# Attention and a Fourier mixing layer on one core: sums made ahead, another rounding instruction, a planner's allowance, and the order of the last products

## The chip, the core and the metric

The kernel runs on one core of a Trainium2 chip. The metric is device time in microseconds. The kernel before was timed three times; a further execution was profiled.

A core has PE (TensorE, matmuls), DVE (VectorE), ACT (ScalarE) and POOL (GpSimd); SP (SyncE) issues the DMAs here. Each engine takes its instructions in order.

## The reference

```python
# A: attention, S = 2048, D = 1024, 32 heads of 32
qkv = (x @ wqkv).reshape(B, S, 3, H, Dh).transpose(2, 0, 3, 1, 4)
scores = einsum("bhqd,bhkd->bhqk", q, k) * Dh ** -0.5
o = einsum("bhqk,bhkd->bhqd", softmax(scores), v)
a = o.transpose(0, 2, 1, 3).reshape(B, S, D) @ wo
# B: Fourier mixing, real part, with given matrices
ar = einsum("bsd,ed->bse", x, dft_hid_re); ai = einsum("bsd,ed->bse", x, dft_hid_im)
y = einsum("ts,bse->bte", dft_seq_re, ar) - einsum("ts,bse->bte", dft_seq_im, ai)
out = concatenate([a, y], axis=-1)
```

All inputs and outputs are float32.

## The kernel before

**Products.** Every large matrix product (q, k and v; dense1 and dense2 for the Fourier part; the projection with `wo`) is cut into 2 x 2 blocks and done with seven block products instead of eight. Each needs sums or differences of blocks as operands; products are numbered 1 to 7. dense1 runs them in the order `OUTER = (1, 2, 5, 6, 7, 4, 3)`; its products 1 and 3 (`SPLIT`) are themselves done with seven inner products. These two are called the split stages. The stationary operands of dense1 are blocks of B_x (`xb`), the moving ones blocks of the sequence matrices (`ct`).

**Rounding.** A float32 operand is split into a rounded part (fp32r, "high") and the rest ("low"), and each product is three matmuls: high x high, low x high, high x low. `halves` (line 543) makes both: the high part with a copy on DVE (line 550, in the trace a CAST) or, where `spare` is set, on ACT (line 549); the low part with a subtraction on POOL or DVE (line 553). `spare` is set in the first five stages of q, k and v (x < 5), in the split stages, and from `behind()` on in the projection. `piece` prepares a stationary operand, `moving` a moving one. `fetch` loads the blocks from DRAM, adds them (line 530, POOL or DVE) and can store the sum.

**Sums.** In dense1, `split_a` names the blocks whose sum a stationary operand is. `simple(p)` loads and adds them at the beginning of product p, when n = 0 (8 operands of 128 x 4 x 128); products 5 and 6 store their sums, since 6 is made from 5, and the third sums (for the split product 3) are made and stored within product 7. `split(i)` loads and adds the operands of its inner products itself, 2 for each.

**Attention.** For each head, scores are made twice: by rows (psS, line 1586), for the maximum (DVE, line 1592) and the sum of exponentials (ACT, line 1595), and transposed (psT, line 1711) for the exponentials that are used (ACT, line 1718) and then multiplied by v (line 1741). The maxima go through DRAM (`m_d`) into the operand of the transposed scores (qs). Attention runs from about 185 to 2762 us; the block products are filled in between its matmuls.

**The planner.** All instructions are recorded as operations with a duration, an engine and sometimes another engine with another duration and rank. At trace time `Plan` runs a clock and gives each engine its next operation by rank; the result is the written order of every engine's instructions. Its costs are constants: CAST 0.415, ACAST (a rounding on ACT) 0.63, ADD 0.68 (an addition on DVE), SUB 1.31 (on POOL). An operation marked `two` and any operation on POOL exclude each other in the plan, and such an order is kept on the chip by an added dependency. `MARGIN` adds to the expected landing of a load before an engine may be given what uses it: POOL 2, DVE 2 (3 while attention runs), ACT 0.

**The projection.** `project` runs its seven products in `ORDER` (1, 2, 7, 6, 5, 3, 4), 8 groups of 12 matmuls each, in slots of SBUF given by `WHERE`. Operands q(r, 0) come from heads 0 to 15, q(r, 1) from heads 16 to 31. `behind()` opens memory that is free only when all heads have been stored; before it, loads use the buffers of the earlier stages.

Of the kernel before, what the change touches and what calls it, by code (L numbers as in the profile page):

```python
# [224 lines left out]
def kernel(  # L225
# [154 lines left out]
    SUB = 1.31  # L380
    ISSUE = 0.46
# [161 lines left out]
    def halves(raw, made, users, hi, lo, old, mine, order=(None, None)):  # L543

        rank = seq()

        def high(e=None):
            if e == "ACT":
                return nc.scalar.activation(hi(), raw(), AF.Copy)
            return nc.vector.tensor_copy(hi(), raw())  # L550

# [3 lines left out]
        a = op("DVE", CAST, high, [made] + old[0], [users, mine[0]], 10 + rank, 0, order[0], ("ACT", ACAST, 25 + rank) if spare[0] else None, two=True)  # L555
# [85 lines left out]
    CR.users = [att_gate for _ in range(NCR)]  # L641

    def qkv():
# [269 lines left out]
        for x, (p, blocks, v) in enumerate(STEPS[:10]):  # L913
# [26 lines left out]
            for t in range(8 if v else 0):  # L940
# [5 lines left out]
                if t < 4 and x < 4:  # L946
                    load_v_weight(x + 1, t)
            where[0] = within
# [8 lines left out]
        for x in (10, 11):  # L957
            for t in range(8):
                v_group(x, t)
                if x == 11 and t < 4:  # L960
# [7 lines left out]
        for b in range(8):  # L968
            W = [piece(w_terms(p, lambda i, j: wqk[b + 8 * i][:, 4 * j : 4 * j + 4, :], None, None)) for p in (7, 4)]
            for n in range(2):  # L970
                qk_group(10, W[0], b, n)
                qk_group(11, W[1], b, n)

# [276 lines left out]
    def dense1():  # L1250
        s4 = [[[] for _ in range(2)] for _ in range(4)]
        t2 = [[[] for _ in range(8)] for _ in range(4)]
        s2 = [[[] for _ in range(2)] for _ in range(4)]
        s2_d = [[dram.tile([P, 4, P], F32, name=f"s2_d{m}_{k}") for k in range(2)] for m in range(4)]
        s4_d = [[dram.tile([P, 4, P], F32, name=f"s4_d{m}_{k}") for k in range(2)] for m in range(4)]
# [3 lines left out]
        s1, t1 = [[[] for _ in range(2)] for _ in range(4)], [[[] for _ in range(8)] for _ in range(4)]  # L1259
        s1_d = [[dram.tile([P, 4, P], F32, name=f"s1_d{m}_{k}") for k in range(2)] for m in range(4)]  # L1260
        t1_d = [[dram.tile([P, NB], F32, name=f"t1_d{n}_{c}") for c in range(8)] for n in range(4)]
        xq = lambda d, s: (xb[d, :, s : s + 4, :], [])
# [6 lines left out]
        def simple(p):  # L1269
            def a(m, k):  # L1270
                q = lambda r, kk: xq(4 * r + m, 8 * kk + 4 * k)
                return split_a(p, q, (s1_d[m][k], s1[m][k]), (s2_d[m][k], s2[m][k]))
# [5 lines left out]
            keep_a = {5: lambda m, k: (s1_d[m][k], s1[m][k]), 6: lambda m, k: (s2_d[m][k], s2[m][k])}.get(p, lambda m, k: None)  # L1278
            keep_b = {5: lambda n, c: (t1_d[n][c], t1[n][c]), 6: lambda n, c: (t2_d[n][c], t2[n][c])}.get(p, lambda n, c: None)
            A = {}  # L1280
            for n in range(4):
# [4 lines left out]
                def load(m, k):  # L1286
                    if n == 0:
                        A[m, k] = held(fetch([P, 4, P], a(m, k), keep_a(m, k)), None if m < 2 else 12 + 2 * m + k)
# [8 lines left out]
                for m in range(4):  # L1297
# [4 lines left out]
                    if p == 7 and 3 in SPLIT and m % 2:  # L1302
# [640 lines left out]
```

## Time and profile before

| | us |
|---|---|
| median of three runs | 2924.29 (2923.43 to 2924.42) |
| profiled execution | 2924.82 |
| its span | 2923.0 |
| PE busy | 2911.5 |
| DVE, ACT, POOL busy | 2260.2, 2297.2, 1107.2 |

The stages, found by counting the block products' matmuls in the trace: first five stages of q, k and v to 206 us (each some 40; stage x = 3 from 124, x = 4 from 162); the rest of q, k and v to 782; dense1's product 1 to 948, 2 to 1143, 5 to 1340, 6 to 1536, 7 to 1732, 4 to 1928, 3 to 2108; dense2 to 2767; the projection's products from then on, 22 us each. A share of busy time is read against such a stretch. The granted clock of PE is 1.00 throughout. A matmul's recorded duration contains its passage through the engine, so matmuls overlap in the record, and PE's rate is read from their starts.

### The profile page before, as it was taken

To read this page: it belongs to the slowest core of one execution; us is meant where nothing else is said; L and a number is where in the kernel's file an instruction comes from. 1 tells how busy PE (TensorE), PEld (TensorE's weight loads), DVE (VectorE), ACT (ScalarE), POOL (GpSimd) and SP (SyncE) were. 2 spreads that over 40 slices of the span, in tenths; PEclk is the share of its full clock that TensorE was granted. 3 is DMA by queue.
4 is the path that set the end of the run, shared out by engine and by line. 5 is a ranking of instruction groups with operands and counts; after the bars stand their busy time and mean duration, and the time that the engine had idled before them with its cause. 6 is when DMAs were issued, how large, how long until landed. Compare 5 with 4: busy or idle time off the path is not lost.

```text
span 2923.0 us, 46116 instructions
## 1 busy us (share of the span) xinstructions
PE 2911.5 (100%) x14826; PEld 2130.8 (73%) x14826; DVE 2260.2 (77%) x3072; ACT 2297.2 (79%) x4369; POOL 1107.2 (38%) x866
## 2 busy tenths in 40 slices
PE   9999999999999999999999999999999999999999
PEld 7887777776667776777776777777677777777787
DVE  7778888788889768777778787778877877876496
ACT  5348888888899888888888888988888888887532
POOL 2323335222365124243434342347613653342042
PEclk9999999999999999999999999999999999999999
DMA  9975658766687448678869775568735776663463
GB/s 340 372 241 186 201 183 280 231 214 223 220 263 227 146 136 274 219 241 273 277 224 286 227 240 170 155 192 281 231 98 172 255 238 189 188 189 123 124 241 140
DMA packets 444956, 636.24 MB, mean 218 GB/s; under 512 B 115726, under 2 KB 150286, under 8 KB 444590
## 3 DMA queue, kind: packets, MB, share of 16 engines
q1 hardware_dynamic: 444716, 633.29, 67.8%
q8 instruction: 120, 1.97, 0.3%
q14 instruction: 120, 0.98, 0.1%
HBM read 448.56 MB, written 184.57 MB: 217 GB/s over the span
## 4 chain that ended last, share of the span: by engine, by line
PE 94%; ACT 2%; DMA 2%; DVE 1%; issue 1%; SPq 0%; DVEq 0%; ACTq 0%
PE pd L433 43%; PE psT L1711 16%; PE psS L1586 15%; PE pd L1741 14%; PE psT L433 6%; ACT psS L1595 1%; ACT pt L1718 1%; DMA qs<-m_d 0%; DMA m_d<-lt 0%; DVE negm L1592 0%; DMA raw<-in_ct 0%; PE psT L455 0%; DMA er<-in_xa 0%; DMA qs<-qk_d 0%; DMA er<-in_wv 0%
## 5 line engine op out<-in xcount | busy, mean ns | idle before, releaser
L1592 DVE TENSOR_REDUCE negm<-psS 128x1 f32<-128x1024 f32 x1024 | 1242.4, 1220 | 255.9 <-PE psS L1586 244.6
L1595 ACT ACTIVATE psS<-psS,negm 128x1024 f32<-128x1024 f32 x1024 | 1230.0, 1201 | 75.2 <-DVE negm L1592 69.5
L1718 ACT ACTIVATE pt<-psT 128x512 f32<-128x512 f32 x1656 | 1000.8, 705 | 267.4 <-PE psT L1711 243.8
L433 PE MATMUL pd<-slot,h 128*128 128x512 f32 x2704 | 921.3, 390 | 0.0
L1711 PE MATMUL psT<-qs,ks 128*128 128x512 f32 x2048 | 794.5, 394 | 2.3 <-ACT pt L1718 1.3
L553 POOL TENSOR_TENSOR slot<-raw,slot 128x512 fp32r<-128x512 f32 x278 | 357.6, 1292 | 776.1 <-DVE slot L550 424.2
L433 PEld LDWEIGHTS pd<-slot,h 128*128 128x128 f32 x2704 | 507.5, 188 | 106.1 <-issue 0.8
L530 POOL TENSOR_TENSOR raw<-raw,g 128x512 f32<-128x512 f32 x321 | 414.8, 1302 | 428.4 <-issue 78.1
L433 PE MATMUL pd<-slot,l 128*128 128x512 f32 x1352 | 526.7, 390 | 0.0
L1711 PEld LDWEIGHTS psT<-qs,ks 128*128 128x128 f32 x2048 | 381.9, 188 | 142.0 <-issue 42.7
L1586 PE MATMUL psS<-ks,qs 128*128 128x512 f32 x1552 | 474.0, 391 | 2.5 <-ACT psS L1595 2.2
L433 PE MATMUL pd<-slot,slot 128*128 128x512 f32 x1560 | 436.3, 389 | 0.0
L1741 PE MATMUL pd<-pt,vt 128*32 128x512 f32 x3312 | 408.2, 594 | 0.0
L1586 PEld LDWEIGHTS psS<-ks,qs 128*128 128x128 f32 x1552 | 290.0, 188 | 67.0 <-ACT psS L1595 6.2
L433 PEld LDWEIGHTS pd<-slot,slot 128*128 128x128 f32 x1560 | 292.8, 188 | 60.8
L1595 ACT ACTIVATION_READ_ACCUMULATOR psS<-psS,negm 128x1 f32 x1024 | 328.2, 321 | 0.0
L433 PEld LDWEIGHTS pd<-slot,l 128*128 128x128 f32 x1352 | 253.8, 188 | 52.3
L1718 ACT ACTIVATE ptm<-psT 128x512 f32<-128x512 f32 x392 | 242.4, 716 | 48.9 <-PE psT L1711 47.1
L1741 PEld LDWEIGHTS pd<-pt,vt 128*32 128x32 f32 x3312 | 108.6, 110 | 231.8 <-issue 217.2
L553 POOL TENSOR_TENSOR l<-raw,h 128x512 fp32r<-128x512 f32 x105 | 135.5, 1290 | 224.5 <-PE psT L1711 79.0
L550 DVE CAST slot<-raw 128x512 fp32r<-128x512 f32 x364 | 168.0, 482 | 6.2 <-DMA raw<-in_wo 3.1
L1586 PE MATMUL psS<-ks,qx 128*128 128x512 f32 x496 | 150.1, 393 | 1.0 <-ACT psS L1595 1.0
(158 smaller groups left out, 2066.0 us busy)
## 6 DMA issues: line engine op xcount, KB each, us to landing
raw<-in_ct SPq DMA_DIRECT2D x212, 256.0 KB
g<-in_ct SPq DMA_DIRECT2D x148, 256.0 KB
raw<-ut_d SPq DMA_DIRECT2D x112, 256.0 KB
qk_d<-e SPq DMA_DIRECT2D x52, 512.0 KB
qs<-qk_d SPq DMA_DIRECT2D x128, 192.0 KB
ks<-qk_d SPq DMA_DIRECT2D x128, 192.0 KB
c<-xx_d SPq DMA_DIRECT2D x80, 256.0 KB
c<-u_d SPq DMA_DIRECT2D x72, 256.0 KB
```

The lines of the kernel that those rows point to most:

```text
L433: nc.tensor.matmul(box["ps"], a[1]((a[0].hi, a[0].lo)[u]()), b[1]((b[0].hi, b[0].lo)[v]()), start=k == 0, stop=k == n - 1)
L530: return (nc.gpsimd if e == "POOL" else nc.vector).tensor_tensor(out=dest(), in0=x, in1=y, op=ALU.add if sign > 0 and not turned else ALU. ...
L550: return nc.vector.tensor_copy(hi(), raw())
L553: return (nc.gpsimd if e == "POOL" else nc.vector).tensor_tensor(out=lo(), in0=raw(), in1=f(hi()), op=ALU.subtract)
L1586: nc.tensor.matmul(p[:, i * NB : i * NB + NB], (QX[0] if own else QS[h % 2])[:, qt * P : qt * P + P], KS[h % 2][:, c * 1024 + i * NB : c * ...
L1592: nc.vector.tensor_reduce(out=ST["negm"][:, c, qt : qt + 1], in_=box["p"], axis=AX.X, op=ALU.max, negate=True)
L1595: nc.scalar.activation(box["p"], box["p"], AF.Exp, bias=ST["negm"][:, c, qt : qt + 1], accum_out=ST["sums"][:, c, qt : qt + 1])
L1711: nc.tensor.matmul(box["p"], KS[h % 2][:, t * P : t * P + P], QS[h % 2][:, j * NB : j * NB + NB], start=True, stop=True)
L1718: nc.scalar.activation(box["t"], box["p"], AF.Exp)
L1741: nc.tensor.matmul(po["p"][j * DH : j * DH + DH, :], VT[h][:, k, :], box["t"], start=(k == t0), stop=(k == t), tile_position=(0, j * DH),)
```

## The change

It does five things.

1. `halves`: where `spare` is set, the high part on DVE is made by a `tensor_reduce` with the maximum over an axis of one element instead of `tensor_copy`. In the plan it costs SLOW = 0.6 and is not marked `two`.
2. `presum` makes a stationary sum of dense1 with `fetch` and stores it in DRAM; `BESIDE` says beside which stage: the 8 of the inner product operands of product 1 beside stage x = 3, the 8 sums of product 5 beside v's products 7 and 4, the 8 of product 6 beside the q and k products 7 and 4, those of 7 and the third ones (16) beside product 2, the inner ones of product 3 (8) beside product 4. `simple` and `split` then load one finished operand.
3. In the projection product 7 goes second. Its operands' differences, which product 6 uses again, go to DRAM (`s7_d`, `t7_d`) and are loaded again; `behind()` comes with the loads of product 2; slots are dealt anew.
4. `MARGIN["ACT"]` is 3 while attention runs, else 0.
5. The separate sums `s1`, `s2`, `s4` and their stores fall away.

```diff
@@ halves
+        one = spare[0]
         def high(e=None):
             if e == "ACT":
                 return nc.scalar.activation(hi(), raw(), AF.Copy)
+            if one:
+                return nc.vector.tensor_reduce(out=hi(), in_=wide(raw()), op=ALU.max, axis=mybir.AxisListType.X)
             return nc.vector.tensor_copy(hi(), raw())
+        def wide(t):
+            return t.rearrange("p (n o) -> p n o", o=1) if len(t.shape) == 2 else t.rearrange("p b (n o) -> p b n o", o=1)
-        a = op("DVE", CAST, high, ..., two=True)
+        a = op("DVE", SLOW if one else CAST, high, ..., two=not one)
@@ new, ahead of qkv
+    def presum(key):
+        what, i, m, k = key
+        if key in sums_of:
+            return
+        if i in (6, 3):
+            presum((what, {6: 5, 3: 6}[i], m, k))
...
+        terms = split_a(i, q, sums_of.get((what, 5, m, k), ()), sums_of.get((what, 6, m, k), ()))
+        to = sums_of[key] = dram.tile([P, 4, P], F32, name=f"sum{what}_{i}_{m}_{k}"), []
+        fetch([P, 4, P], terms, to)
+    BESIDE = {"x":of_inner(1),"v":of_all(5),"qk":of_all(6),2:of_all(7)+of_all(3),4:of_inner(3)}
@@ simple
+                if p in (5, 6, 7, 3):
+                    presum(("s", p, m, k))
+                    return [(1, *sums_of["s", p, m, k])]
...
-                    if p == 7 and 3 in SPLIT and m % 2:
-                        i, k = divmod(2 * n + m // 2, 2)
-                        fetch([P, 4, P], [(1, *xq(i, 8 + 4 * k)), (-1, s2_d[i][k], s2[i][k])], (s4_d[i][k], s4[i][k]))
+                    beside(p, 1)
@@ project
-                6: lambda: [(1, A22[j][c]), (-1, S2[j][c])],
+                6: lambda: [(1, A22[j][c]), (-1, *S7[j][c])],
-        ORDER = (1, 2, 7, 6, 5, 3, 4)
+        ORDER = (1, 7, 2, 6, 5, 3, 4)
-                    Y[i // 2] = accs(12 + i // 2)
+                    Y[i // 2] = accs(g[1] + i // 2)
-                    if n != 2:
+                    if n == 2:
+                        behind()
+                        load_a(n, J0 + J1)
+                    elif n != 7:
                         load_a(n, J0)
                 if x == i == 0:
-                    load_a(2, J0 + J1)
+                    load_a(7, J0)
@@ the plan's loop
+        pl.MARGIN["ACT"] = 3 if heads and t_on[0] else 0
```

## Rows read from the trace of the kernel before

**Rows 1.** The page, part 1: busy us (share of the span) xinstructions

```profile
PE 2911.5 (100%) x14826; PEld 2130.8 (73%) x14826; DVE 2260.2 (77%) x3072; ACT 2297.2 (79%) x4369; POOL 1107.2 (38%) x866
```

**Rows 2.** The chain that ended last, its end: start us, us, what

```profile
2911.16 5.44 PE pd L433 x24
2916.60 2.73 PE psT L433 x12
2919.36 0.42 DVE e L1050
```

**Rows 3.** All waits of PE: who, awaited, us in total, times, longest us

```profile
PE psS L1586 <- ACT psS L1595: 3.2, 9, 0.6
PE pd L1817 <- DVE qs L312: 1.5, 1, 1.5
PE psT L1711 <- ACT pt L1718: 1.3, 2, 1.1
PE psT L1711 <- DMA qs<-m_d: 0.8, 2, 0.5
PE psT L455 <- DVE acc L821: 0.7, 1, 0.7
```

**Rows 4.** Timeline: start us, us, instruction, idle before it and releaser

```profile
717.36 0.63 ACT L549 ACTIVATE slot<-raw 128x512 fp32r<-128x512 f32 x1 [0.76 <-DMA raw<-in_ct]
718.52 0.50 PE L1711 MATMUL psT<-qs,ks 128*128 128x512 f32 x1 [0.27 <-ACT pt L1718]
...
799.61 0.63 ACT L549 ACTIVATE slot<-raw 128x512 fp32r<-128x512 f32 x1 [1.50 <-DMA raw<-in_ct]
800.78 0.50 PE L1711 MATMUL psT<-qs,ks 128*128 128x512 f32 x1 [1.08 <-ACT pt L1718]
```

**Rows 5.** Casts on DVE: dense1 products 1 and 3, then line 550 min/median/max

```profile
L550 DVE CAST slot<-raw 128x512 fp32r<-128x512 f32 x32 | 14.6, 479 | 0.9 <-DMA raw<-in_ct 0.9
...
L550 DVE CAST slot<-raw 128x512 fp32r<-128x512 f32 x39 | 19.8, 526 | 0.0
...
L550 DVE CAST slot<-raw x364: 382/419/1375, 188.3 to 2743.6; 128x512 fp32r<-128x512 f32 x182
```

**Rows 6.** Reductions on DVE and an addition on POOL: duration of one

```profile
L1592 DVE TENSOR_REDUCE negm<-psS 128x1 f32<-128x1024 f32 x1024 | 1242.4, 1220 | 255.9 <-PE psS L1586 244.6
...
L1619 DVE TENSOR_REDUCE lh<-negm x32: 178/186/189, 235.8 to 2686.5; 128x16 fp32r<-128x32 f32 x32
...
L530 POOL TENSOR_TENSOR raw<-raw,g x321: 1269/1289/1788, 259.9 to 2670.2; 128x512 f32<-128x512 f32 x161
```

**Rows 7.** Timeline before stage x=4: a weight load, an addition

```profile
136.18 0.43 SPq L511 DMA_DIRECT2D er<-in_wqk  x1
...
154.68 0.68 DVE L530 TENSOR_TENSOR er<-er,raw 128x512 f32<-128x512 f32 x1
```

**Rows 8.** Busy us by stretch: length, PE PEld DVE ACT POOL, clock, DMA, GB/s

```profile
124.00:162.00 38.00, 38.00 (x169) 31.49 (x168) 25.25 (x33) 11.58 (x19) 11.50 (x9) 1.00 0.86 310
162.00:205.00 43.00, 43.00 (x191) 35.60 (x190) 32.80 (x44) 16.73 (x29) 6.41 (x5) 1.00 0.75 250
782.00:948.00 166.00, 164.84 (x842) 119.04 (x841) 145.27 (x208) 152.12 (x293) 106.03 (x84) 1.00 0.78 242
1928.00:2108.00 180.00, 178.67 (x941) 125.28 (x940) 151.37 (x208) 158.03 (x306) 118.63 (x93) 1.00 0.81 254
2686.00:2767.00 81.00, 81.00 (x455) 54.80 (x454) 31.55 (x65) 40.17 (x75) 1.28 (x1) 1.00 0.36 110
2767.00:2788.00 21.00, 21.00 (x94) 17.38 (x94) 12.34 (x18) 8.84 (x14) 5.59 (x4) 1.00 0.88 306
2788.00:2810.00 22.00, 22.00 (x98) 17.93 (x97) 21.86 (x29) 8.84 (x16) 8.96 (x7) 1.00 1.03 370
```

**Rows 9.** The chain around a transfer of a head's maxima

```profile
550.79 5.50 DMA m_d<-lt
```

**Rows 10.** Waits of PE within dense1's product 3, 1928 to 2108 us

```profile
PE psS L1586 <- ACT psS L1595: 1.3, 4, 0.6
```

More of the change, by code (lines that the diff above doesn't have):

```diff
@@ L549, in high @@
                 return nc.scalar.activation(hi(), raw(), AF.Copy)
+            if one:
+                return nc.vector.tensor_reduce(out=hi(), in_=wide(raw()), op=ALU.max, axis=mybir.AxisListType.X)
             return nc.vector.tensor_copy(hi(), raw())
+        def wide(t):
+            return t.rearrange("p (n o) -> p n o", o=1) if len(t.shape) == 2 else t.rearrange("p b (n o) -> p b n o", o=1)
         def low(e):
             return (nc.gpsimd if e == "POOL" else nc.vector).tensor_tensor(out=lo(), in0=raw(), in1=f(hi()), op=ALU.subtract)
-        a = op("DVE", CAST, high, [made] + old[0], [users, mine[0]], 10 + rank, 0, order[0], ("ACT", ACAST, 25 + rank) if spare[0] else None, two=True)
+        a = op("DVE", SLOW if one else CAST, high, [made] + old[0], [users, mine[0]], 10 + rank, 0, order[0], ("ACT", ACAST, 25 + rank) if spare[0] else None, two=not one)
         b = op("POOL", SUB, low, [a] + old[1], [users, mine[0], mine[1]], rank, 0, order[1], other=("DVE", ADD, 25 + rank), two=True)
@@ L641, with of_all, of_inner, beside @@
     CR.users = [att_gate for _ in range(NCR)]
+    xq = lambda d, s: (xb[d, :, s : s + 4, :], [])
+    sums_of = {}
+    def presum(key):
[4 more added lines that the diff above has]
+            presum((what, {6: 5, 3: 6}[i], m, k))
+        if what == "s":
+            q = lambda r, kk: xq(4 * r + m, 8 * kk + 4 * k)
+        else:
+            q = lambda r, kk: sums_of["s", 3, 2 * r + m, kk] if what == 3 else xq(2 * r + m, 8 * (what - 1) + 4 * kk)
+        terms = split_a(i, q, sums_of.get((what, 5, m, k), ()), sums_of.get((what, 6, m, k), ()))
+        to = sums_of[key] = dram.tile([P, 4, P], F32, name=f"sum{what}_{i}_{m}_{k}"), []
+        fetch([P, 4, P], terms, to)
+    def of_all(p):
+        return [("s", p, m, k) for m in range(4) for k in range(2)]
+    def of_inner(i, ps=(5, 6, 7, 3)):
+        return [(i, p, n, 0) for p in ps for n in range(2)]
+    BESIDE = {"x":of_inner(1),"v":of_all(5),"qk":of_all(6),2:of_all(7)+of_all(3),4:of_inner(3)}
+    def beside(what, n):
+        todo = BESIDE.get(what, [])
+        for key in todo[:n]:
+            presum(key)
+        del todo[:n]
     def qkv():
@@ L959, in qkv @@
                 v_group(x, t)
+                if t % 2:
+                    beside("v", 1)
                 if x == 11 and t < 4:
@@ L972, in qkv @@
                 qk_group(11, W[1], b, n)
+                beside("qk", 1)
     ORDER = (1, 2, 6, 7, 5, 3, 4)
@@ L1502, in project @@
         T2 = [kept(f"t2_{c}") for c in range(4)]
+        S7 = [[(dram.tile([P, NB], F32, name=f"s7_d{j}_{c}"), []) for c in range(4)] for j in range(2)]
+        T7 = [(dram.tile([P, NB], F32, name=f"t7_d{c}"), []) for c in range(4)]
         def load_b(p):
             for c in range(4):
-                B[p, c] = moving(WHERE[p][1] + c, b_terms(p, c), None, T2[c] if p in (6, 7) else None)
+                B[p, c] = moving(WHERE[p][1] + c, b_terms(p, c), T7[c] if p == 7 else None, T2[c] if p == 6 else None)
         def load_a(p, which):
```

40 lines of the change are left out of this document (18 added, 22 removed).

## Prediction

> **What bounds the kernel now.** The page's first part comes first: PE (the matrix engine) is busy for 2911.5 of 2923.0 us [rows 1]. The change alters neither the number nor the shape of the matmuls, so it can win no more than PE's idle time, 2923.0 - 2911.5 = 11.5 us. Next, the end of the chain [rows 2]: the last matmul ends at 2916.60 + 2.73 = 2919.33, and 3.7 us of evacuation and storing follow, the same two half-tile steps after the change. The list of PE's waits [rows 3] has 1.5 us before the first matmul, also unchanged, and 6.0 us in 14 waits. A wait costs more than its idle time: a matmul is recorded for 0.390 us, but 24 of them take 5.44 us in the chain [rows 2], 0.227 each, so a wait moves the next start by its idle time and 0.163 more. The 14 waits cost 6.0 + 14 x 0.163 = 8.3 us; one of them, 0.7 + 0.16 on an accumulator, is in the first 20 us, which the change leaves alone. What is left, 7.4 us, is the most that this change can return: 0.25% of the time. Of these 13 waits 11 are on ACT (3.2 us for score exponentials, 1.3 for the transposed ones), two on a small DMA. So the question of each edit is which of these waits it takes away, and whether it makes one of its own.
>
> **Allowance on ScalarE.** Two waits can be followed to their cause in the timeline [rows 4]. At 799.61 ACT starts a rounding after standing idle for 1.50 us until that tile's load lands; the exponential queued behind it is late, and PE waits 1.08 us at 800.78. At 717.36 the same with 0.76 us, and PE waits 0.27. Both are roundings of dense1's product 1, taken by ACT at the very moment at which the planner expected the load. With MARGIN 3 the planner gives ACT such a tile only 3 us after the expected landing, more than either lateness. The gain is 1.08 + 0.27 + 2 x 0.163 = 1.7 us at most, nothing at worst (DVE, which already has an allowance, gets the tile, and its maxima stand ahead of the same exponentials). I take 1.7, for the cause is visible in both rows.
>
> **Rounding as a maximum over one element.** In the stages where ACT may help (`spare`), DVE's cast becomes a TENSOR_REDUCE. It applies to 45 casts in 782 to 948 us and to 49 in 1928 to 2108, of which [rows 5] show the two largest groups (32 at 479 ns, 39 at 526; the rest lie in smaller groups of 419 to 500), and to 13 in the first 205 us. A cast left alone takes 419 ns, but up to 1375 [rows 5]: it has to wait while POOL works. The reduce that reads SBUF was never over 189 ns in 32 cases [rows 6], so it does not wait for POOL. Its price for 512 outputs is not in the trace. From 1220 ns for 1024 elements and 186 for 32 [rows 6], one element costs 1034 / 992 = 1.04 ns, so 512 cost 186 + 480 x 1.04 = 0.69 us. The bounds are 0.42 (a cast alone) and 1.22 (a reduce of twice the input); I take 0.69, which is also nearest to an addition with 512 outputs, 0.68 us [rows 7]. DVE then has 45 x (0.69 - 0.48) = 9.5 us more in product 1, 145.3 + 9.5 = 154.8 of 166, and 49 x (0.69 - 0.51) = 8.8 more in product 3, 151.4 + 8.8 = 160.2 of 180 [rows 8]. Both still fit, so I cost it at nothing on PE. In return POOL's additions and subtractions (1.29 us each [rows 6]) can run beside a rounding.
>
> The Trainium skill speaks against this edit: "VectorE: DVE Perf Modes", section "Rules for kernel authors", says to expect the single rate of `tensor_reduce` and to restructure around it. By that rule alone DVE only loses, nothing of the 1.0 us that I count below for product 3 would come, and the time would be 2923.1. The page "SBUF — State Buffer", section "SBUF: two separate sides", has the counterweight: DVE's two-port modes and GpSimd exclude each other. The cast's spread of 382 to 1375 ns agrees with it.
>
> **Sums made ahead.** 48 sums of B_x blocks were made where they are used; now each is made earlier, stored, and loaded when used. The additions stay 48, but 8 of them leave each split stage: 8 x 1.29 = 10.3 us of POOL's 106.0 and 118.6 us there [rows 8], and 12 transfers leave each as well. In all, 56 transfers of 256 KB are added (8 loads each for the sums of products 5 and 6, 8 stores and 8 loads for product 7's, 12 for each split product; product 3's outer sums were stored and loaded before too), 14.7 MB. The full rate is 370 GB/s [rows 8], 0.71 us each. Most of it goes into stages with room. The tight place is the first: 8 sums for product 1 go into 124 to 162 us, 24 transfers or 17.0 us on top of 0.86 x 38 = 32.7, which overfills the stretch by 11.7 us; the next has 0.75 x 43 = 32.3 and takes it up to 44.0 of 43. Those loads go ahead of stage x = 4's weight blocks in the ring of load buffers. The last such block is loaded at 136.18, and the last addition on one runs at 154.68 [rows 7], so some 15 us of lead cover 17 of delay. I cost it at 0.2 us, between 0 and 5 (nothing else is ready for PE at 162). Elsewhere a busier queue lengthens small transfers on which PE waits, such as a head's maxima, 5.50 us at 550.79 [rows 9]; the two DMA waits, 0.8 us idle in all [rows 3], may grow by 0.2.
>
> What ACT, DVE and POOL get back in the split stages should show in product 3, where PE has 4 waits on ACT with 1.3 us idle [rows 10]: 1.3 + 4 x 0.163 = 1.95 us. ACT is only 158.0 of 180 us busy there, but in runs of exponentials without a gap, which fewer roundings on ACT break up only in part. Bounds 0 and 1.95; I take half, 1.0.
>
> **Product 7 second in the projection.** Both first products now use heads 0 to 15 alone, so 43 us of matmuls rather than 22 cover the last heads' store and load. But PE had no wait there: busy 21.00 of 21 and 22.00 of 22 [rows 8]. The gain is nothing. The cost: products 1 and 7 are prepared before `behind()`, so without ACT's roundings (8.84 us in 2767 to 2788). By 2788 DVE and POOL must do 12 casts, 12 low parts and 8 subtractions, 12 x 0.42 + 20 x 0.69 = 18.8 us if DVE does all, beside 8 evacuations of 0.69: 24.3 us in the 26 after attention ends near 2762. Before that they are little used (31.55 and 1.28 of 81). It just fits, and POOL takes some; I cost it at 0.1, between 0 and 3. In exchange DVE, which was full at 2788 to 2810 (21.86 of 22), has product 2's plain roundings there. The 12 stores and 12 reloads of S7 and T7 (17 us of transfers) fall where DMA has room and before product 6.
>
> **The sum.** -1.7 - 1.0 + 0.2 + 0.2 + 0.1 = -2.2 us. The profiled execution took 2924.82 us, 1.8 more than its span; it becomes 2922.6. The median of the three runs lies 0.5 below the profiled one: 2922.1.
>
> **Rivals.** *The waits are only dealt anew.* The planner places all later instructions again once a cost changes; waits go here and come there, or DVE's maxima come later by what ACT's exponentials gain. For it: 5 of the 11 waits on ACT lie outside both sets of rows, with no edit near. Time 2924.3, give or take 2.5. This is also where the change does not do what it says. *All waits go.* POOL and ACT have slack enough that nearly all of the 7.4 us vanish, 2917. Against it: the waits outside the split stages have other causes. *The one-element maximum is dear.* In the split stages, DVE is full when a rounding takes 0.48 + 20.7 / 45 = 0.94 us in product 1 (166 - 145.3 = 20.7 free) or 0.51 + 28.6 / 49 = 1.09 in product 3. At 1.22 it overruns by 45 x 0.74 - 20.7 = 12.6 and 49 x 0.71 - 28.6 = 6.2 us; if ACT's slack takes half, PE loses 9.4: slower, 2922.1 + 9.4 = 2931.5. Only a price for each output makes it so; the two reduces, with 1 and 16 outputs, hardly tell, and the addition with 512 speaks against it. *The run-up in the first stage* at its bound, 5 us, gives 2927.
>
> **How the numbers follow.** Forecast 2920 to 2924: 0.50. Dealt anew, 2922 to 2927: 0.25. All waits go: 0.12. Dear maximum: 0.08. Run-up: 0.05. The range leaves out half of the third and all of the fourth: 2917 to 2928. 0.2%, about what a measurement of this kernel can tell from no change, is 5.8 us: faster means under 2918.4, slower over 2930.1. Faster 0.11, same 0.80, slower 0.09.
>
> **What would show it.** In the changed profile: the waits at 717 and 800 gone and no ACT rounding with idle time on a DMA in attention; TENSOR_REDUCE on line 550's successor at 0.6 to 0.7 us without spread; POOL busy in product 1 and 3 about 10 us less; DMA near full from 124 to 205 with PE at 43.00 of 43; no wait of PE after 2767. It is wrong if the reduce is over 0.9 us, if PE waits near 162 or 2788, or if as many waits on ACT stand elsewhere.

## The result and the profile after

The change makes the kernel slower by 0.2%: 2930.95 us (median of 13 runs, 2927.28 to 2935.98) against 2925.45 for the kernel before, run beside it (13 runs, 2922.22 to 2942.39). The ratio is 1.002, 95% interval 1.0011 to 1.0028. The forecast was 2922.1 in a range of 2917 to 2928; the time lies outside it.

The profiled execution took 2933.52 us, 2.6 more than the median; its span is 2931.5, 8.5 more than before. Lines have moved: the block products' matmuls are on 434 and 456 (433 and 455 before), psS on 1629, psT on 1754, the product with v on 1784, the reduction for rounding on 553, the cast on 554, ACT's rounding on 551, the low part on 560. Part 1 of the page of the changed kernel, to be held against [rows 1]:

```profile
PE 2915.4 (99%) x14826; PEld 2131.0 (73%) x14826; DVE 2257.3 (77%) x3079; ACT 2277.8 (78%) x4326; POOL 1150.0 (39%) x902
```

The number of matmuls is the same. PE's idle time has gone from 11.5 to 2931.5 - 2915.4 = 16.1 us, and its busy time is up by 3.9, so matmuls also ran slower. Where it waits, beside [rows 3] (all waits of PE in the changed kernel: who, awaited, us in total, times, longest):

```profile
PE psS L1629 <- ACT psS L1638: 3.6, 5, 1.3
PE psT L1754 <- DMA qs<-m_d: 3.2, 2, 1.8
PE pd L1860 <- DVE qs L312: 1.5, 1, 1.5
PE pd L1784 <- DVE e L794: 1.4, 1, 1.4
PE psT L434 <- POOL l L560: 0.8, 1, 0.8
PE psT L434 <- ACT h L551: 0.8, 1, 0.8
PE psT L456 <- DVE acc L860: 0.4, 1, 0.4
PE psT L434 <- DVE l L560: 0.3, 1, 0.3
```

The two waits on transposed exponentials are gone, and the nine on score exponentials are five, though longer ones (3.6 us in all, 3.2 before). New are three waits within the first block products (L434), one in the product with v (L1784), and the two on a head's maxima have grown from 0.8 to 3.2 us.

**At 162 us.** The beginning of stage x = 4 in the timeline of the changed kernel (start, us, instruction, idle time before it and its releaser):

```profile
154.11 0.67 SPq L512 DMA_DIRECT2D er<-in_wqk  x1
154.83 0.77 SPq L521 DMA_DIRECT2D raw<-sum  x1
...
161.38 0.69 DVE L531 TENSOR_TENSOR er<-er,raw 128x512 f32<-128x512 f32 x1
162.10 0.63 ACT L551 ACTIVATE h<-er 128x512 fp32r<-128x512 f32 x1 [14.62 <-DVE er L531]
162.79 0.49 PE L434 MATMUL psT<-slot,h 128*128 128x512 f32 x1 [0.77 <-ACT h L551]
164.13 0.50 PE L434 MATMUL psT<-slot,l 128*128 128x512 f32 x1 [0.85 <-POOL l L560]
```

A weight block is issued at 154.11. Before, the last three of this stage were issued at 132.53, 133.58 and 136.18 (the last: [rows 7]); now they come at 154.11, 156.73 and 162.14, 22 to 26 us later. So the addition on it runs at 161.38, the rounding at 162.10, and PE waits for that rounding, then for its low part. The windows of the changed kernel tell why, and what follows (length; PE, PEld, DVE, ACT, POOL busy; granted clock; DMA share; GB/s):

```profile
124.00:162.00 38.00, 38.00 (x168) 31.17 (x166) 19.61 (x30) 5.41 (x9) 10.48 (x8) 1.00 0.97 341
162.00:209.00 47.00, 45.08 (x190) 36.48 (x190) 35.63 (x50) 20.31 (x34) 16.63 (x13) 0.96 0.93 332
165.00:169.00 4.00, 4.00 (x12) 3.13 (x12) 1.52 (x3) 1.02 (x2) 1.28 (x1) 0.62 1.06 406
480.00:539.00 59.00, 57.58 (x315) 37.93 (x314) 46.03 (x58) 46.62 (x88) 31.92 (x25) 1.00 0.97 322
539.00:586.00 47.00, 45.22 (x222) 33.20 (x221) 36.58 (x49) 39.68 (x78) 20.41 (x16) 1.00 0.93 304
787.00:952.00 165.00, 165.00 (x845) 119.47 (x843) 152.37 (x212) 146.12 (x282) 109.23 (x87) 1.00 0.71 227
1937.00:2104.00 167.00, 164.89 (x849) 117.12 (x848) 147.04 (x197) 143.15 (x276) 114.61 (x91) 1.00 0.81 255
```

DMA is at 0.97 and 0.93 where it was at 0.86 and 0.75 [rows 8]. And in the four microseconds behind the two waits the granted clock is 0.62 on average: the clock's record has half the clock, the 1.2 GHz level, from 164.65 on for 3.41 us. PE, which had run without a gap until 162, had just stood idle twice within 2 us. Eight matmuls then start every 0.427 us instead of 0.227: 1.6 us more. Stage x = 4 ends at 209.3 instead of 205.6.

**In the stages of v.** In the fourth and fifth line above v's products 7 and 4 are done; that is where the eight sums of dense1's product 5 are now made. In the kernel before, the same two stages read:

```profile
475.00:534.00 59.00, 59.00 (x307) 42.70 (x296) 48.31 (x61) 50.09 (x96) 29.86 (x24) 1.00 0.84 281
534.00:580.00 46.00, 45.66 (x225) 34.24 (x225) 34.61 (x46) 40.18 (x79) 13.46 (x11) 1.00 0.77 241
```

DMA went from 0.84 to 0.97 and from 0.77 to 0.93, PE lost 1.42 and 1.78 us. The first loss, in the timeline of the changed kernel:

```profile
527.00 0.33 SPq L824 DMA_DIRECT2D c<-u_d  x1
...
530.17 0.69 DVE L794 TENSOR_TENSOR e<-c,pd 128x512 f32<-128x512 f32 x1 [2.56 <-DMA c<-u_d]
...
530.91 2.35 PE L1784 MATMUL pd<-pt,vt 128*32 128x512 f32 x20 [1.38 <-DVE e L794]
```

The list of waits names DVE, but DVE had itself been waiting 2.56 us for a transfer: the partial sum `c`, read back from DRAM, lands late. DVE's addition frees the accumulator that the product with v needs next. The second loss is the wait for the maxima at 569.46 (1.75 us).

**In the projection.** No wait is left there. But its end in the chain of waits of the changed kernel (compare [rows 2], 5.44 us for 24 matmuls) reads:

```profile
2809.27 5.44 PE pd L434 x24
2814.71 5.53 PE psT L434 x24
2820.24 5.60 PE pd L434 x24
2825.84 5.56 PE psT L434 x24
2831.40 5.44 PE pd L434 x24
```

The same 24 matmuls take 5.53 to 5.60 us in a part of the products, with the clock at 1.00 and nothing awaited. By starts of matmuls, half a product (48) takes 10.88 us, but in products 2, 6, 3 and 4 one half takes 11.20: it is always the half whose stationary operand lies in slot 12. The half behind it takes 10.92. The projection takes 153.75 us; it was 152.57.

**The account.** From start to start of matmuls, changed minus before: the waits and the lower clock at 162 to 178, +4.4 (by the stage's end, 3.7); waits on maxima, +2.5; the wait in the product with v, +1.4; the projection's pitch, +1.4; small differences of under 0.03 us from one start to the next in the other stages, +1.2; waits on ACT in attention, -2.3. That is 8.6 of the 8.5.

This is the account of one execution; between the medians there are 5.5 us. Traces of other kernels that make the same sums beside the same stages show how much of it varies. The stretch from 140 to 213 us of the kernel before, by the same matmuls, is 4.0 us longer in the changed kernel, 4.1 in e2 below, but 1.9 in e4 and e14, where the waits in it are two of 0.5 to 0.6 us each; only the changed kernel has half clock there. In the stages of v, PE stands idle for 1.4 and 1.8 us in the changed kernel (L1784 and the maxima), 1.2 and 1.6 in e2, 1.4 and 2.1 in e4, 1.8 and 2.3 in e14.

### The profile page after: what moved, and what is told of

Same layout as the page of the kernel before. It is cut to its first block, busy times and chain, and to the rows that moved or that the text cites. A ratio compares the mean times of both kernels' runs of the same rounds, so it can differ in the third digit from the quotient of the medians.

```text
span 2931.5 us, 46241 instructions
## 1 busy us (share of the span) xinstructions
PE 2915.4 (99%) x14826; PEld 2131.0 (73%) x14826; DVE 2257.3 (77%) x3079; ACT 2277.8 (78%) x4326; POOL 1150.0 (39%) x902
## 4 chain that ended last, share of the span: by engine, by line
PE 91%; DMA 5%; DVE 2%; SPq 1%; issue 0%; ACT 0%; POOL 0%; DVEq 0%; ACTq 0%; POOLq 0%
PE pd L434 41%; PE psT L1754 15%; PE psS L1629 15%; PE pd L1784 15%; PE psT L434 5%; DMA c<-u_d 1%; DVE negm L1635 1%; DMA w_d<-raw 0%; DMA raw<-sums 0%; DMA er<-in_xb 0%; DMA sum<-er 0%; DMA sq_d<-er 0%; DMA qs<-qk_d 0%; DMA er<-in_xa 0%; DMA raw<-in_ct 0%
## 5 line engine op out<-in xcount | busy, mean ns | idle before, releaser
L1638 ACT ACTIVATE psS<-psS,negm 128x1024 f32<-128x1024 f32 x1024 | 1215.3, 1187 | 75.6 <-DVE negm L1635 70.1
L1761 ACT ACTIVATE pt<-psT 128x512 f32<-128x512 f32 x1656 | 989.8, 693 | 273.6 <-PE psT L1754 251.2
L434 PE MATMUL pd<-slot,h 128*128 128x512 f32 x2704 | 919.7, 390 | 0.0
L560 POOL TENSOR_TENSOR slot<-raw,slot 128x512 fp32r<-128x512 f32 x301 | 387.2, 1292 | 780.5 <-DVE slot L554 484.3
L434 PEld LDWEIGHTS pd<-slot,h 128*128 128x128 f32 x2704 | 507.6, 188 | 105.8 <-issue 0.8
L434 PE MATMUL pd<-slot,l 128*128 128x512 f32 x1352 | 526.6, 390 | 0.0
L434 PE MATMUL pd<-slot,slot 128*128 128x512 f32 x1584 | 445.0, 390 | 0.0
L1784 PE MATMUL pd<-pt,vt 128*32 128x512 f32 x3312 | 408.2, 594 | 1.4 <-DVE e L794 1.4
L434 PEld LDWEIGHTS pd<-slot,slot 128*128 128x128 f32 x1584 | 297.4, 188 | 61.5
L1629 PEld LDWEIGHTS psS<-ks,qs 128*128 128x128 f32 x1552 | 289.5, 188 | 69.1 <-ACT psS L1638 10.1
L1638 ACT ACTIVATION_READ_ACCUMULATOR psS<-psS,negm 128x1 f32 x1024 | 312.3, 305 | 0.0
L434 PEld LDWEIGHTS pd<-slot,l 128*128 128x128 f32 x1352 | 253.8, 188 | 52.5 <-POOL l L560 0.2
L1784 PEld LDWEIGHTS pd<-pt,vt 128*32 128x32 f32 x3312 | 108.5, 110 | 233.4 <-issue 217.4
L560 POOL TENSOR_TENSOR l<-raw,h 128x512 fp32r<-128x512 f32 x115 | 148.3, 1290 | 242.8 <-PE psT L1754 98.3
L554 DVE CAST slot<-raw 128x512 fp32r<-128x512 f32 x312 | 146.9, 489 | 6.0 <-DMA raw<-in_wo 2.9
```

The costliest lines, as they stand in the source:

```text
L434: nc.tensor.matmul(box["ps"], a[1]((a[0].hi, a[0].lo)[u]()), b[1]((b[0].hi, b[0].lo)[v]()), start=k == 0, stop=k == n - 1)
L560: return (nc.gpsimd if e == "POOL" else nc.vector).tensor_tensor(out=lo(), in0=raw(), in1=f(hi()), op=ALU.subtract)
L1629: nc.tensor.matmul(p[:, i * NB : i * NB + NB], (QX[0] if own else QS[h % 2])[:, qt * P : qt * P + P], KS[h % 2][:, c * 1024 + i * NB : c * ...
L1638: nc.scalar.activation(box["p"], box["p"], AF.Exp, bias=ST["negm"][:, c, qt : qt + 1], accum_out=ST["sums"][:, c, qt : qt + 1])
L1761: nc.scalar.activation(box["t"], box["p"], AF.Exp)
L1784: nc.tensor.matmul(po["p"][j * DH : j * DH + DH, :], VT[h][:, k, :], box["t"], start=(k == t0), stop=(k == t), tile_position=(0, j * DH),)
```

## The experiments

Each series ran on one chip beside the kernel before, whose median in it is given. "Sums" is part 2 of the change, "order" part 3.

**The parts by themselves** (before: 2925.43 for the first two, 2925.47 for the next two, 2924.79 for the last).

e2_sums_alone: the kernel before with `presum`, `BESIDE` and the loads of finished sums, nothing else.

> The kernel before with the sums made ahead, and nothing else of the change. Theory (the transfers of the sums cost the time): PE waits near 162 us by 1 to 2 us with a half-clock stretch behind it, waits on the maxima's transfer (qs<-m_d) are longer than before's 0.5 and 0.2, and the kernel is 4 to 8 us slower than before. Rival (the other edits cost it): no wait near 162 us, within 2 us of before.

e3_without_sums: the whole change without that part.

> The changed kernel without the sums made ahead: rounding as maximum, allowance on ACT and the projection's order stay. Theory (the transfers of the sums cost the time): no wait near 162 us, full clock, and 1 to 3 us faster than before, less 1.3 us in the projection if the slots there cost something. Rival (rounding or order cost it): still 3 us or more slower than before.

e7_rounding_alone: only the new instruction in `halves`.

> The kernel before with the rounding as one-element maximum alone. Theory (it fits, since DVE is not full): a reduce takes 0.68 us whether POOL works or not, within 2 us of before, and ACT does fewer roundings in the split stages. Rival (DVE is late by it): waits of PE on DVE or on ACT in the split stages, 3 us or more slower.

e8_allowance_alone: only this line.

```diff
+        pl.MARGIN["ACT"] = 3 if heads and t_on[0] else 0
```

> The kernel before with the allowance on ACT alone. Theory: the two waits near 718 and 801 us that come of a rounding on ACT waiting for its load are gone, no rounding on ACT waits for a transfer between 300 and 2700 us, 1 to 2 us faster than before. Rival (the plan is dealt anew): as many waits of PE on ACT as before in other places, no difference beyond 1 us.

e12_order_alone: only the projection's part, with its slots.

> The kernel before with product 7 second in the projection alone. Theory: everything before the projection as before, the wait of the third half product (11.13 us before) gone, -0.25 us, and four half products at 11.2 us in place of 10.88, +1.3 us: 1 us slower than before in the projection, 2926.5. Rival (preparing product 7 without ACT is late): waits of PE in product 7, 2 us or more slower.

| | median us | ratio to before (95%) |
|---|---|---|
| e2 sums alone | 2935.56 | 1.0032 (1.0019 to 1.0045) |
| e3 without sums | 2926.60 | 1.0003 (0.9993 to 1.0012) |
| e7 rounding alone | 2925.77 | 1.0002 (0.9993 to 1.0011) |
| e8 allowance alone | 2926.93 | 1.0005 (0.9996 to 1.0013) |
| e12 order alone | 2926.61 | 1.0005 (0.9996 to 1.0014) |

The loss is in the sums; each of the other parts is no different from before that can be measured. The intervals are some 5 us wide, so they show neither a gain of 1 to 2 us nor that there is none; the 1 to 3 us that e3 was to be faster can't be seen.

e2 loses 10.1 us, more than the 4 to 8 expected and more than the whole change, but its interval and that of the change (1.0011 to 1.0028) overlap. Its waits near 165 us (1.3, 0.8, 0.9) and in the stages of v are there as expected; the half clock expected behind the first is not, and stands at 1998 instead, behind a wait of 2.6 us on ACT.

In e8 the two waits of [rows 4] are gone, as the forecast had it. Of PE's waits in attention and dense1 this line is left (e8):

```profile
PE psS L1586 <- ACT psS L1595: 4.0, 9, 0.7
```

Before, 13 waits of 5.3 us stood there [rows 3]. Those on the transposed exponentials (1.3) and on a head's maxima (0.8) went; those on the scores went from 3.2 to 4.0, at other places (2059 to 2098, 2326). With 0.163 for each wait that is 7.4 before and 5.5 now, so in this trace attention gains 1.9 us, near the 1.7 forecast. But outside attention, where the allowance is 0, the accumulator's wait is 0.6 us longer and one of 0.5 stands at 2790, PE's idle time is 11.3 us after 11.5, and the median shows no gain. So the cause was read rightly; whether the time gains by it these runs can't tell. e12 (2926.5 expected) and e3 both have the projection's 153.75 us with halves of 11.20, so its pitch belongs to part 3. In e12 the one wait that the projection had before, 0.25 us at 2790 by starts of matmuls and too short for [rows 3], is gone, which gives that much back.

**Where the sums are made** (before: 2925.43, 2925.47, and 2923.83 for e13 and e16).

e1_inner_sums_later: the sums for product 1 beside stages x = 7 and 8 instead of x = 3.

```diff
+                if x in (7, 8):
+                    beside("x", 1)
...
-                if x == 3:
-                    beside("x", 1)
```

> The changed kernel with one move: the 8 inner sums of dense1's product 1 are made beside the stages x = 7 and 8 instead of beside x = 3. Theory (transfers run up ahead of stage x = 4): the weight blocks of x = 4 are again loaded near 133 us, the two waits at 162.8 and 164.1 us (0.77 and 0.85 idle) and the 3.4 us at half clock behind them are gone, stage x = 3 of q, k, v to x = 4 takes 44 us again, and the time falls by about 4 us, to within 0.1% of the kernel before. Rival (the new rounding instruction on DVE is late in that stage): the waits near 162 us stay, and the time stays 5 us over the kernel before.

e5_inner_sums_at_use: those sums are made within product 1, as before the change.

```diff
-    BESIDE = {"x":of_inner(1),"v":of_all(5),"qk":of_all(6),2:of_all(7)+of_all(3),4:of_inner(3)}
+    BESIDE = {"v":of_all(5),"qk":of_all(6),2:of_all(7)+of_all(3),4:of_inner(3)}
...
+                    if i == 1:
+                        A.append(piece(split_a(j, lambda r, k: xq(2 * r + n, 4 * k), at(5, n), at(6, n)), at(j, n) if j in (5, 6) else None))
```

> The changed kernel, except that the inner sums of dense1's product 1 are made where they are used, as before; all other sums stay made ahead. Theory (the run-up of transfers ahead of stage x = 4 is one cost among others): no wait and no half clock near 162 us, some 4 us less than the changed kernel's 2931 us, near 2927; the waits that the other sums bring between 480 and 590 us (one of 1.4 us before the products with v, one of 1.8 us on the maxima's transfer) stay. Rival (the early run-up is all of it): 2925 or less, no wait over 0.5 us between 480 and 590 us.

e16_sums_beside_qk: e5, and the sums of product 5 are made together with those of 6 beside the last q and k products, none beside v.

```diff
-    BESIDE = {"v":of_all(5),"qk":of_all(6),2:of_all(7)+of_all(3),4:of_inner(3)}
+    BESIDE = {"qk":of_all(6),2:of_all(7)+of_all(3),4:of_inner(3)}
```

> The changed kernel with the inner sums of product 1 made where used, and the sums of product 5 made beside the q and k stage, together with those of 6 (16 sums there, none beside the two stages of v). Theory (the stages of v, whose transfers the sums fill to 0.97, cost): no wait of the products with v on DVE near 527 us, the maxima's transfer near 560 us waited for 1 us or less, and 2 us faster than with the sums beside v (e5, 2929.7). Rival (the stage of q and k, with its loads of earlier sums, costs as much): as slow as e5, with a wait of the products with v on DVE near 714 us of 1.5 us or more.

e6_sums_late_slots_shifted: e5, and no sum before dense1 (those of 5 and 6 beside product 2, of 7 beside 5, the third ones beside 6); the late buffers, slot 12 of the projection among them, lie 32 bytes further.

```diff
+    BESIDE = {2:of_all(5)+of_all(6),5:of_all(7),6:of_all(3),4:of_inner(3)}
...
+            late["op"].tile([P, 8], F32, name="pad")
```

> The changed kernel with the inner sums of product 1 made where they are used and the other sums made one product before their use within dense1 (5 and 6 beside product 2, 7 beside 5, the third ones beside 6), so none while q, k and v are made; and 32 bytes of nothing ahead of the projection's memory, so that slots 12 to 15 begin 32 bytes later. Theory (the sums cost only where the transfers are full): no wait near 162 us, no wait of the products with v on DVE near 485 us, about as fast as the changed kernel without the sums (2926.6) or 1 to 2 us faster; rival (sums cost wherever they are): as slow as 2930. For the slots: if the matmuls there are slow by the parity of their 32-byte place, all half products of the projection now take 10.88 us; if by the region of memory, four of them still take 11.2.

e13_sums_late_shift96: the same with 24 elements, 96 bytes.

> As e6 (inner sums of product 1 made where used, the others one product before use within dense1), but with 96 bytes instead of 32 ahead of the projection's memory, so that slots 12 to 15 begin at byte 49120, which leaves the same remainder by 256 as all other operands' places. Theory (same remainder by 256 is fast): all 14 half products take 10.88 us, four of them 0.11 less than in e6, and the time is 0.5 us below e6's 2924.1, near 2923.6, 1 to 2 us faster than before. Rival (the region below 64 KB is slow): four half products stay at 11.0 to 11.2.

| | median us | ratio to before (95%) |
|---|---|---|
| e1 inner sums beside x = 7, 8 | 2938.08 | 1.0043 (1.0031 to 1.0056) |
| e5 inner sums at use | 2929.70 | 1.0016 (1.0007 to 1.0025) |
| e16 also none beside v | 2925.48 | 1.0008 (0.9999 to 1.0017) |
| e6 all in dense1, 32 bytes | 2924.14 | 0.9997 (0.9988 to 1.0006) |
| e13 all in dense1, 96 bytes | 2923.40 | 1.0001 (0.9992 to 1.0010) |

e1 was to show that only the tight place at 162 costs, and it refutes that: no wait is left there, but moved to stages that had looked emptier, the sums cost more. Stage x = 7 in the kernel before, then in e1, then eight microseconds of it in e1 (windows as above):

```profile
301.00:360.00 59.00, 59.00 (x305) 42.89 (x304) 47.38 (x68) 49.72 (x98) 20.92 (x18) 1.00 0.66 206
301.00:363.00 62.00, 59.10 (x291) 40.21 (x290) 44.95 (x63) 50.71 (x99) 24.40 (x20) 0.97 0.79 252
310.00:318.00 8.00, 5.10 (x16) 2.31 (x14) 7.68 (x14) 7.04 (x15) 3.60 (x3) 0.98 1.01 364
```

The stage has DMA at 0.79 on average, and PE loses 2.9 us of it in a stretch where DMA is full. Two of e1's waits, in the list of PE's waits:

```profile
PE psS L1629 <- ACT psS L1638: 6.6, 6, 2.4
PE pd L434 <- DVE l L560: 1.9, 1, 1.9
```

The second is at 317.04, in the block products, and the clock is at half behind it from 317.7 on for 3.41 us. It falls twice more in e1, at 481.5 and 546.4, at waits of 1.9 and 2.4 us. The loads for a sum go into the ring of load buffers ahead of the stage's own.

e5 takes the sums out of the first stages altogether. From 162 to 206 PE is full again, and DMA is back at 0.83 and 0.74; beside v it is as crowded as in the changed kernel (windows of e5):

```profile
124.00:162.00 38.00, 38.00 (x170) 31.45 (x169) 24.88 (x33) 11.05 (x19) 10.71 (x9) 1.00 0.83 302
162.00:206.00 44.00, 44.00 (x196) 36.32 (x195) 33.79 (x44) 17.68 (x29) 6.43 (x5) 1.00 0.74 247
476.00:535.00 59.00, 57.80 (x318) 39.02 (x318) 46.21 (x60) 48.40 (x91) 29.30 (x23) 1.00 0.97 322
535.00:582.00 47.00, 47.00 (x237) 35.15 (x239) 37.21 (x51) 41.36 (x82) 20.43 (x16) 1.00 0.95 310
```

In the medians that returns little (1.0016 after 1.002): 2929.70, where 2927 was expected. The wait in the product with v at 527 is there (1.1 us), the one on maxima near 569, also expected to stay, is not, and the second stage has PE full at a DMA share of 0.95. New are waits of 1.5 us in the product with v at 714 and 0.8 on maxima at 401. e16 frees the stages of v too (windows of e16, the same two stages):

```profile
476.00:535.00 59.00, 59.00 (x301) 43.33 (x300) 49.37 (x63) 51.33 (x98) 30.79 (x25) 1.00 0.84 277
535.00:582.00 47.00, 47.00 (x252) 33.01 (x251) 32.91 (x45) 39.95 (x78) 15.88 (x13) 1.00 0.87 273
```

DMA is at 0.84 and 0.87, PE full, and e16 is 4.2 us under e5 (2.6 when each is held against its own before; the intervals of the two ratios overlap). What stays is mostly the projection's pitch: the same sums in dense1, with the operands placed better, e6 and e13, equal the kernel before within the measurement. They move 11.5 MB more than e15, which makes no sums ahead, where the change moves 14.7; the additions are 500 in each of these kernels, so no run prices them.

A full DMA need not cost anything: the kernel before has two of its first stages at 1.00 and 1.03 with PE full:

```profile
45.00:85.00 40.00, 39.98 (x177) 32.74 (x176) 32.09 (x42) 16.80 (x29) 13.00 (x11) 1.00 1.00 363
85.00:124.00 39.00, 39.00 (x174) 32.30 (x173) 28.14 (x42) 13.47 (x23) 9.85 (x8) 1.00 1.03 375
```

In the places followed above the loss comes where a load on which PE's next matmuls hang lands late: a weight block at 162, the partial sum at 530, the maxima at 569. The first two are the sums': waits near 165 stand in the four traces with sums beside x = 3 and in no other, one of 1.1 to 1.8 us near 530 in five of the six with sums beside v (not in e1) and in no other. The third is not shown to be theirs. It is 1.6 to 2.3 us in the four, but e1 and e5, with sums beside v, have none, and without sums there it varies between executions of kernels that differ in the projection alone: none in e13, 1.0 in e6 and 1.8 at 560 in e10, with DMA at 0.73:

```profile
535.00:582.00 47.00, 45.20 (x228) 33.44 (x230) 34.38 (x46) 39.76 (x78) 12.16 (x10) 1.00 0.73 226
```

**The projection's pitch** (before: 2925.43 for e4, 2924.79 for e9 to e11, 2923.83 for e14 and e15).

e4_slot12_moving: the slots hold moving operands in 12 and stationary ones elsewhere.

```diff
-            1: ([24, g[1]], g[0]), 7: ([g[2], g[0]], 24), 2: ([12, 20], g[2]), 6: ([24, 12], g[0]),
-            5: ([20, 24], g[2]), 3: ([12, 20], g[0]), 4: ([24, 12], g[2]),
+            1: ([24, g[1]], g[0]), 7: ([g[2], g[0]], 24), 2: ([20, g[2]], 12), 6: ([24, g[0]], 20),
+            5: ([g[2], 24], 12), 3: ([g[0], g[2]], 20), 4: ([24, g[0]], 12),
```

> The changed kernel with other slots in the projection: slots 12 to 15, which hold stationary operands of products 2, 6, 3 and 4 there, hold only moving ones. Theory (matmuls whose stationary operand lies in slots 12 to 15 start every 0.2333 instead of 0.2267 us): no product of the projection takes more than 21.8 us, against 22.1 for four of them, and the stretch from the projection's first matmul to its last falls by 1.3 us, from 153.8 to 152.5. Rival (whatever lies in these slots is slow, also as moving operand): products 2, 5 and 4 take over 22 us. Rival (it was chance in that execution): no pattern by slot. The waits near 162 us stay.

2932.64 us, 1.0020 (1.0012 to 1.0029). Both halves of the products with slot 12 (now 2, 5 and 4) take 11.24 us, and the projection 154.5. So it is not the weight load: an operand in slot 12 slows the product in either role. The 152.5 us expected were wrong.

e9_matmul_places: the layer is left out; groups of 12 matmuls of the same shapes on operands at chosen places, 30 pairs.

> Not the layer at all: 30 times 48 matmuls of the projection's form (128 x 128 stationary, 512 columns moving, rounded float32), each time with the two operands at another place in SBUF, everything else left out; its output is filler. The projection's slots 12 to 15 begin at byte 49024 of a partition, its others at 114656 or higher, and all others are odd multiples of 32. Theory by parity (both operands at odd multiples of 32 are fast): 49056 with 180192 takes 0.2267 us a matmul, 49024 with 180192 0.233, in either role. Theory by region (operands far apart or in the lower part are slow): 49024 and 49056 alike 0.233 with 180192 and fast with 32768. Rival (no effect of place, the projection's slow halves come from other traffic): all pairs 0.2267.

The mean from start to start, in ns (byte of the stationary operand, byte of the moving one; the first two pairs ran in part at half the clock and are left out):

```
114656 180192 227.2    114656 196576 227.3    114656  32800 228.8
114688  32768 227.3    114688 180224 226.8    114688  81920 227.2
 49056 180192 229.1
 49024 180192 233.5     49024 180224 232.5     49024 196576 233.2
114656 180224 233.4    114688 180192 233.2    180192  49024 233.9
all others 232.4 to 234.3
```

Pairs whose two addresses leave the same remainder by 256 (224: 114656, 180192, 196576; 0: 114688, 32768, 81920, 180224) run at 0.227, nearly all others at 0.233. In the kernel all large operands leave 224, except slot 12 of the projection at 49024, which leaves 128. Like remainders other than 224 and 0 were not tried. Two pairs at 228.8 and 229.1 don't fit this rule or one by regions of memory; 49056 with 196576, whose remainders are those of 49056 with 180192, takes 233.3.

The 32 bytes of e6 put slot 12 at 49056; its four half products took 10.99 us there, 48 x 0.229, as 49056 with 180192 does in the table. 96 bytes put it at 49120, which leaves 224.

e14_change_shift96: the change with the late buffers 96 bytes further.

```diff
+            late["op"].tile([P, 24], F32, name="pad")
```

> The changed kernel with 96 bytes ahead of the projection's memory and nothing else. Theory: half products of 10.88 us, 1.3 us less than the changed kernel's 2931, so 2929.6; the waits near 162 us and their half clock stay. Rival: half products of 11.2 stay.

e15_no_sums_shift96: the same without the sums.

> The changed kernel without the sums made ahead, with 96 bytes ahead of the projection's memory. Theory: half products of 10.88 us, 1.3 us less than without the shift (2926.6), 2925.3, the same as before within the measurement: rounding, allowance and order together win nothing. Rival (they win on ACT what they were meant to): 2923 or less.

In e14, as in e13 and e15, every half product takes 10.88 us and the projection 152.32, 1.4 less than in the changed kernel. The end of e14's chain, at the place of the fence above:

```profile
2809.66 5.44 PE pd L434 x24
2815.10 5.44 PE psT L434 x24
2820.54 5.44 PE pd L434 x24
2825.98 5.44 PE psT L434 x24
```

e14's median is 2929.49, 1.0017 (1.0009 to 1.0026): with its early waits still there (0.62 at 167.6, 0.53 at 187.65; the half clock that was expected there is not), 1.8 us in the product with v at 528 and 2.3 on maxima at 567, it stays slow. e15 takes 2922.46, 0.9998 (0.9989 to 1.0007), the lowest median of all and within its rival's "2923 or less", but not told apart from before. e13, e14, e15 and the kernel before ran side by side: the sums where the change puts them cost 2929.49 - 2922.46 = 7.0 us, made in dense1 2923.40 - 2922.46 = 0.9, which is within the measurement. e15's waits of PE on ACT and on maxima:

```profile
PE psS L1597 <- ACT psS L1606: 1.9, 4, 0.6
PE psT L1722 <- DMA qs<-m_d: 1.9, 2, 1.5
PE psT L1722 <- ACT pt L1729: 0.9, 1, 0.9
```

Two attempts to leave slot 12 out by loading the second half's operands later in the same slots:

e10_sums_late_no_slot12, with the sums in dense1:

> The changed kernel with the inner sums of product 1 made where they are used, the other sums one product before their use in dense1, and no operand of the projection in slots 12 to 15 (they rotate through the four sets g0, g2, 20 and 24). Theory (the costs of the change are the transfers beside q, k and v and the slots; its gains on ACT stay): no wait near 162 or 485 us, projection 152.5 us, 1 us less than with shifted slots (2924.1), so near 2923, 2 us faster than before. Rival (the rest of the change costs as much as it gains): 2925 or more.

e11_no_sums_no_slot12, without them:

> The changed kernel without the sums made ahead, and no operand of the projection in slots 12 to 15. Theory (slots cost 1.3 us): 1.3 us faster than the kernel with those slots (2926.6), near 2925.3, and the projection takes 152.5 us. Rival: the projection stays at 153.7.

2928.89, 1.0015 (1.0006 to 1.0024), and 2929.06, 1.0018 (1.0009 to 1.0027): both miss. The pitch is 10.88, but the operands of one half come too late; in e10's timeline:

```profile
2856.28 0.97 PE L434 MATMUL psT<-slot,slot 128*128 128x512 f32 x3 [1.09 <-POOL slot L560]
2858.85 0.73 PE L434 MATMUL psT<-slot,slot 128*128 128x512 f32 x2 [1.60 <-POOL slot L560]
```

In e11 the same two waits (1.12, 1.58) are followed by 3.41 us at half the clock, in e10 by none. The half product takes 15.80 us in e11 and 14.16 in e10, so this half clock costs 1.6.

## Why the prediction was wrong, point by point

- **The bound** held for the gain: PE sets the time, and of the 7.4 us nothing measurable was won. The waits on ACT in attention fell by 2.3 us where 1.7 + 1.0 had been counted. But the sum took PE's busy time as given since the matmuls are the same, and it rose by 3.9 us, most of it by the half clock (1.6) and the operands' places (1.4).
- **The allowance** did what it was to do at 717 and 800; product 1 has PE at 165.00 of 165, and no ACT rounding waits for a load in attention. In product 3 ACT's four waits of [rows 10] became one of 0.6 us: 1.3 + 4 x 0.163 - 0.6 - 0.16 = 1.2 us, where 1.0 was taken. But a wait of 1.4 us on maxima (1993) stands there now; one at 1986 (1.7) also stands in e3, without sums.
- **The one-element maximum** was right: 0.69 us forecast. By the view of its line in the changed kernel (min/median/max ns):

```profile
L553 DVE TENSOR_REDUCE slot<-raw x75: 668/676/689, 715.6 to 2884.1; 128x512 fp32r<-128x512 f32 x75
```

  Of 119 such reductions 97 ran while POOL worked, at 677 ns like the rest; the casts still reach 1510. So the rival of the dear maximum falls.
- **POOL ten microseconds less in the split stages** did not come: 109.2 and 114.6 us, beside 106.0 and 118.6 in [rows 8]. The planner gave POOL other work instead: it has 87 and 91 instructions there, and had 84 and 93.
- **The run-up in the first stage** is the first step that failed. It stood at 0.2 us with a bound of 5; it cost 3.7 by the stage's end in the profile, 1.9 in e4 and e14. The delay was 22 to 26 us instead of 17 against 15 of lead, and the lead was not a cover: two waits of 0.8 us, with a lower clock behind them that alone cost 1.6. Such a price stood nowhere in the sum. Mended by itself (e5) it returned 1.2 us in the medians, which the measurement can't tell from nothing; other waits came with the new order.
- **"Most of it goes into stages with room"** is the second. The stages of v were called roomy without a row of their own. They were at 0.84 and 0.77, and 24 transfers brought them to 0.97 and 0.93. The 0.2 us stood for the maxima alone; they grew by 2.5, but neither the wait at 569 (1.75; 1.8 in e10 without the sums) nor the one at 1993 can be laid to the sums for certain. A second chain, partial sum from DRAM, DVE, product with v, was not seen (1.4), and that one is theirs. e16, without this part, shows PE full there. And e1 shows that a stage's average share, by which the prediction reckons room, doesn't tell: 0.66 before, and PE lost 2.9 us.
- **Slots dealt anew** were costed at nothing, as an edit that moves no work: 1.4 us by the place of operands (e14).
- **The second product of the projection** was right: no wait after 2767. The kernel before did have one, of 0.25 us, which busy shares of 22.00 in 22 had hidden.
- **The rival "dealt anew"** fits the times of each small part by itself (e7, e8, e12), which as well fit a gain of 1 us. The changed kernel goes past it because the sums add real costs.

So the forecast failed by its costs: 0.5 us were set for the sums' transfers and the order, and the sums made where the change puts them cost 7.0 us (e14 against e15), the places of operands 1.4. Left open: how the 7.0 us divide between the stages, why the waits on maxima near 560 and at 1986 to 1993 come and go with and without the sums, what the 1.2 us of small differences are, and e5's and e16's distance, which the runs give only as 2.6 to 4.2 us.

## What to carry to other kernels

A transfer that is moved is priced at the stage that takes it: its own DMA share, its ring of load buffers, and each chain in it that goes through DRAM and back. The average share of a stage is not enough for it: here PE lost nothing at 1.03 in one stage and 0.95 in another, lost 1.4 in one at 0.97, 1.8 in one at 0.73 and 2.9 in one at 0.79. In the places followed here what counted was whether a load that PE's next matmuls hang on came late. A wait on a matrix engine that never waits should be priced with the clock that may drop behind it, and an operand given another place with the pitch that its address may bring.

## What the runs showed of the hardware

- A 128x128 by 128x512 fp32r matmul started every 0.227 us or every 0.233, by where its two operands lie relative to each other in SBUF: the same remainder by 256 bytes gave the first in e9, all but two of the others the second. Why, and why 49056 with 180192 and 114656 with 32800 lie between, was not tried.
- At waits of PE of some 1 to 2.6 us, single or two close together, the granted clock fell in some cases to half for 3.41 us: at 164.65 in the changed kernel (two waits of 0.8), 317.7, 481.5 and 546.4 in e1 (1.9, 1.9 and 2.4), 1132.7 in e14 (1.9), 1998.1 in e2 (2.6), 2859.1 in e11 (1.1 and 1.6). It cost 1.6 us where it was counted. In other cases it did not fall: 2.3 us at 567 in e14, 2.1 at 1781 in e16, 1.8 at 569 in the changed kernel, 1.1 and 1.6 at the same place in e10. What decides it stays open.
- A reduction over an axis of one element takes 677 ns for 512 outputs beside POOL's work or without it; a cast of the same size, 380 to 1510, and all 82 over 600 ns overlap an instruction on POOL (changed kernel).
- DMA engines busy for the whole of a stage (1.00 and 1.03 from 45 to 124 us of the kernel before) did not by themselves hold PE up.
